# Landing times of loads in a list scheduler, priority for the first batch, and keys loaded ahead of w_out

## The chip, the cores and the metric

The kernel runs on one core of a Trainium2 chip. Times are device microseconds (us) of one execution; "median" is over several executions. A profile is one execution. The engines are TensorE (PE in the profile; PEld is its weight load), VectorE (DVE), ScalarE (ACT), GpSimd (POOL) and SyncE (SP, which issues most loads).

## The reference, cut to what matters

Sketched linear attention of 4 batches, 4 heads, 1088 tokens, head width 32, whose output feeds an MoE-like layer of width 2048 with a rational activation:

```python
def phi(x):                      # q and k: [4, 4, 1088, 32], S1 and S2: [8, 32]
    a = np.einsum('rd,bhsd->bhsr', S1, x)
    b = np.einsum('rd,bhsd->bhsr', S2, x)
    return np.einsum('bhsi,bhsj->bhsij', a, b).reshape(*x.shape[:-1], r * r)
kv = np.einsum('bhsf,bhsd->bhfd', k_p, v);  z = np.sum(k_p, axis=2)
num = np.einsum('bhsf,bhfd->bhsd', q_p, kv)
den = np.einsum('bhsf,bhf->bhs', q_p, z)[..., None] + 1e-06        # x = num / den
...
h = x @ w_in                     # x: [4352, 128], w_in: [128, 2048]
P = a[0] + a[1] * h + a[2] * h2 + a[3] * h3
Q = 1.0 + np.abs(b[0]) * np.abs(h) + np.abs(b[1]) * h2
out = (P / (Q + 1e-06)) @ w_out
```

Nothing of the MoE can start before the first x, and the first x needs the key sums kv of a whole batch.

## The kernel before

Every piece of work is a step with an engine, a guessed duration, what it waits for, a rank, and the buffers it takes and gives back. A small list scheduler plays the steps through and then issues all instructions in the order of the starts that it found. That order is the order of every engine's queue. The guessed times have no other effect; what a step really waits for is settled on the chip.

```python
HOP = 200
...
        t = free_at.get(s["engine"], 0)
        for a in s["after"]:
            t = max(t, a["end"] + (a["lag"] if a["engine"] == s["engine"] else self.HOP + a["lag"]))
        ...                                        # buffers
        key = (t, s["rank"], s["n"])
        if best is None or key < best[0]:
            best = (key, s)
...
def load(fn, ns, n=1, queue="SP", **kw):
    return plan.add(queue, 500 * n, fn, lag=ns, **kw)

ld["kr"] = load(lambda: load_rem(k_rem, k, nc.scalar), 2500, 4, queue="ACT", rank=-98)
...
ld["vr"] = load(lambda: load_rem(v_rem, v, nc.sync), 2500, 4, rank=-95)
ld["ab"] = load(load_ab, 14000, 2, rank=-93)
ld["wi"] = load(lambda: nc.sync.dma_start(out=w_in_sb, in_=moe_w_in), 8000, rank=-92)
ld["wo"] = load(lambda: nc.sync.dma_start(out=w_out_f, in_=...), 9000, rank=-91, take=["L"])
for i, (name, src) in enumerate((("k", k), ("v", v), ("q", q))):       # batch 1
    ld[name, 1] = load(lambda name=name, src=src: load_main(name + "_sb", src, 1), 6000, rank=-90 + i,
                       take=[name + "_sb"])
```

In the head (before the MoE) TensorE also runs matmuls of zeros between the real ones ("warm"). POOL copies v into v_aug (v beside a column of ones) and converts w_out to bf16. In the MoE each group of 128x512 blocks of h goes through eight DVE steps: m = |h|, u = b1*m + b0, u *= m, y = a3*h + a2, y *= h, y += a1, y *= h, y *= r.

## Time and profile before

Median 309.33 us (308.29, 309.33, 309.43). The execution that was profiled took 312.64; its span is 310.9.

| stretch of the profiled execution | length | DVE busy | granted TensorE clock |
|---|---|---|---|
| head, to the first MoE step m<-hb | 41.58 | 9.68 | 0.79 |
| the rest | 269.32 | 258.73 | 0.95 |

First the page of the kernel before. A digit is the busy share of one fortieth of the span in tenths; PEclk is the granted TensorE clock in tenths.

```profile
span 310.9 us, 3191 instructions
PE   7879999999999998998999899989999699866471
DVE  0503269899999999999999999999999999999991
PEclk9995589999999999999999799999999779979667
```

The digits of the last line begin right behind its label. DVE is nearly full from the seventh slice (of 7.8 us) to the last but one, and the clock is at half in the fourth and fifth. So the kernel is bound by DVE after 41.6 us, and everything before is a chain of latencies.

The wait in the head, from the timeline of the kernel before (start, duration, engine, line, operation, output<-input; in brackets the engine's idle time before it and what ended it):

```profile
10.93 0.76 SPq L177 DMA_DIRECT2D L<-in_moe_w_out_dram  x1
11.73 4.59 SPq L138 DMA_DIRECT2D k_sb<-in_k_dram  x1
...
19.86 0.27 ACT L367 COPY kv_low<-kv_ps 64x132 f32<-64x132 f32 x1 [2.33 <-PE kv_ps L358]
20.44 0.58 ACT L271 COPY fT<-w_ps 128x512 f32<-128x512 f32 x1 [0.32 <-PE w_ps L266]
23.21 0.58 ACT L271 COPY fT<-w_ps 128x512 f32<-128x512 f32 x1 [2.19 <-PE w_ps L266]
23.82 0.30 ACT L374 COPY kv_dup<-kv_dup 64x132 f32<-64x132 f32 x1
...
22.52 1.09 PE L266 MATMUL w_ps<-ident,k_sb 128*128 128x128 f32 x8 [2.12 <-DMA k_sb<-in_k_dram]
23.85 1.97 PE L276 MATMUL w_ps<-S_102,fT 128*128 128x64 f32 x8 [0.24 <-ACT fT L271]
25.61 1.92 PE L414 MATMUL h_ps<-kv_dup,q_pT 128*128 128x66 f32 x8
...
41.58 0.43 DVE L494 TENSOR_SCALAR m<-hb 128x1024 int16<-128x1024 int16 x1 [3.53 <-ACT hb L490]
```

The keys of batch 1 (k_sb) are issued behind w_out, and the issue itself blocks SP's queue for 4.59 us. They land at 22.5. In ScalarE's queue the copy of their transposes (fT, 23.21) stands ahead of the last copy into kv_dup (23.82), which batch 0's num/den matmuls (25.61) need. TensorE's queue holds them up further: the transposes (22.52) and the first projection (23.85) of batch 1's keys stand ahead of num/den, which start 1.5 us after kv_dup is done. So batch 0 waits for batch 1's data twice: the scheduler, which guessed a landing 6 us after issue, thought that they were there.

The clock in that time, from windows of the same trace (start:end, length, then busy time and instruction count of PE, PEld, DVE, ACT, POOL, the granted clock, the DMA share and GB/s):

```profile
20.00:24.00 4.00, 1.65 (x13) 1.17 (x11) 0.36 (x2) 1.47 (x4) 0.00 (x0) 0.94 1.12 329
24.00:28.00 4.00, 4.00 (x19) 3.91 (x20) 1.59 (x3) 0.88 (x3) 1.14 (x2) 0.50 0.89 270
36.00:40.00 4.00, 4.00 (x9) 2.23 (x9) 0.63 (x2) 0.27 (x1) 0.00 (x0) 0.50 0.00 0
```

TensorE had little to do from 20 to 24 us, and its clock was at 0.50 from 24 to 40. The Trainium skill says in "TensorE: Matmul & The Clock Gate" (Part 1, the HAM clock gate) that the clock is halved by default and released by activity, in free-running windows of about 3.4 us. This trace agrees with the two levels and with the fall after a thinly used stretch.

### The profile page before, as it was taken

The page shows a single profiled execution, that of the slowest core. Times are in us where ns is not written, and L with a number is a line of the kernel's source. Part 1 is how long each engine was busy: PE and PEld are TensorE (multiplying, and loading weights), DVE is VectorE, ACT ScalarE, POOL GpSimd, SP SyncE. Part 2 cuts the span into 40 slices and gives each one's busy share as a digit, 9 for nine tenths or more (in the row PEclk, how much of TensorE's full clock was granted, in tenths as well). Part 3 has the DMA queues.
Part 4 walks back from the last instruction along what each step waited for, and adds up shares of the span by engine and source line. Part 5 has one row for each costly group of instructions (what it writes and reads, how often), then busy time and mean ns, then how long its engine had stood idle before and what let it go on. Part 6 is the DMA issues. An engine that isn't in the chain of part 4 may idle for free.

```text
span 310.9 us, 3191 instructions
## 1 busy us (share of the span) xinstructions
PE 276.9 (89%) x1247; PEld 166.6 (54%) x1247; DVE 268.4 (86%) x233; ACT 234.4 (75%) x248; POOL 11.0 (4%) x26
## 2 busy tenths in 40 slices
PE   7879999999999998998999899989999699866471
PEld 3769745665546564664546357645645444543150
DVE  0503269899999999999999999999999999999991
ACT  3222259759999888979995899597987996899460
POOL 3103300010000000000000000000000000000000
PEclk9995589999999999999999799999999779979667
DMA  7699100000200000000000000000000000000010
GB/s 215 166 325 300 61 0 3 1 0 0 70 0 34 2 0 34 0 2 0 34 0 2 0 34 3 0 0 34 3 0 0 34 2 0 34 0 0 0 36 17
DMA packets 12655, 11.22 MB, mean 36 GB/s; under 512 B 4065, under 2 KB 10977, under 8 KB 12513
## 3 DMA queue, kind: packets, MB, share of 16 engines
q1 hardware_dynamic: 11472, 10.88, 11.2%
q10 hardware_dynamic: 1168, 0.14, 0.3%
q8 instruction: 10, 0.16, 0.2%
q14 instruction: 5, 0.03, 0.0%
HBM read 8.79 MB, written 2.23 MB: 35 GB/s over the span
## 4 chain that ended last, share of the span: by engine, by line
DVE 67%; PE 12%; ACT 6%; issue 5%; DMA 5%; SPq 2%; DVEq 0%
DVE y L521 20%; DVE y L528 10%; DVE u L504 9%; DVE y L517 6%; DVE y L524 6%; DVE u L500 5%; DVE m L494 5%; PE h_ps L484 4%; DVE f_p L291 4%; DMA k_sb<-in_k_dram 3%; PE out_ps L535 3%; ACT L L508 2%; DMA v_sb<-in_v_dram 2%; DVE x_sb L441 2%; PE w_ps L276 1%
## 5 line engine op out<-in xcount | busy, mean ns | idle before, releaser
L484 PE MATMUL h_ps<-xT,w_in_sb 128*128 128x512 f32 (+1 forms) x288 | 131.9, 596 | 0.2
L490 ACT CAST hb<-h_ps 128x1024 bf16<-128x1024 f32 x68 | 67.6, 1017 | 22.7 <-PE h_ps L484 22.7
L484 PEld LDWEIGHTS h_ps<-xT,w_in_sb 128*128 128x128 f32 x288 | 55.4, 201 | 47.0 <-issue 39.7
L521 DVE TENSOR_TENSOR y<-y,hb 128x4096 bf16<-128x4096 bf16 (+2 forms) x42 | 78.9, 1879 | 0.2
L508 ACT ACTIVATE L<-u,one_ap 128x2048 f32<-128x2048 bf16 (+1 forms) x36 | 69.2, 1921 | 6.4 <-DVE u L504 6.3
L513 ACT ACTIVATE r<-L 128x2048 bf16<-128x2048 f32 (+1 forms) x36 | 65.8, 1827 | 0.5
L535 PE MATMUL out_ps<-r,w_out_103 128*128 128x512 bf16 (+1 forms) x144 | 36.2, 380 | 9.5 <-ACT r L513 9.3
L535 PE MATMUL out_ps<-y,w_out_104 128*128 128x512 bf16 (+1 forms) x144 | 37.0, 403 | 7.9 <-DVE y L528 7.9
L528 DVE TENSOR_TENSOR y<-y,r 128x4096 bf16<-128x4096 bf16 (+2 forms) x21 | 39.5, 1879 | 1.0 <-ACT r L513 0.9
L504 DVE TENSOR_TENSOR u<-u,m 128x4096 bf16<-128x4096 bf16 (+2 forms) x21 | 39.5, 1879 | 0.0
L291 DVE TENSOR_TENSOR f_p<-a_t,w_ps 128x1024 f32<-128x1024 f32 (+1 forms) x16 | 18.9, 1182 | 15.0 <-ACT a_t L283 15.0
L535 PEld LDWEIGHTS <-w_out_103 128*128 128x128 bf16 x144 | 14.7, 103 | 28.3 <-issue 18.4
L535 PEld LDWEIGHTS <-w_out_104 128*128 128x128 bf16 x144 | 15.1, 107 | 25.1 <-issue 14.7
L494 DVE TENSOR_SCALAR m<-hb 128x4096 int16<-128x4096 int16 (+2 forms) x21 | 21.4, 1018 | 3.5 <-ACT hb L490 3.5
L517 DVE TENSOR_SCALAR y<-hb,a_sb 128x4096 bf16<-128x4096 bf16 (+2 forms) x21 | 23.9, 1138 | 0.0
L500 DVE TENSOR_SCALAR u<-m,b_abs 128x4096 bf16<-128x4096 bf16 (+2 forms) x21 | 23.9, 1137 | 0.0
L524 DVE TENSOR_SCALAR y<-y,a_sb 128x4096 bf16<-128x4096 bf16 (+2 forms) x21 | 22.6, 1078 | 0.2
L276 PEld LDWEIGHTS w_ps<-S_102,fT 128*128 128x128 f32 x128 | 17.9, 209 | 4.4 <-issue 2.1
L276 PE MATMUL w_ps<-S_102,fT 128*128 128x64 f32 x128 | 18.4, 290 | 0.8 <-DVE f_p L291 0.6
L336 PEld LDWEIGHTS kv_ps<-v_aug,f_p 128*128 128x128 f32 x128 | 15.8, 192 | 2.4 <-issue 1.6
L414 PEld LDWEIGHTS w_ps<-kv_dup,q_pT 128*128 128x128 f32 x112 | 14.7, 202 | 4.3 <-issue 2.6
L336 PE MATMUL kv_ps<-v_aug,f_p 128*128 128x66 f32 x128 | 15.6, 271 | 0.0
(77 smaller groups left out, 181.4 us busy)
## 6 DMA issues: line engine op xcount, KB each, us to landing
v_sb<-in_v_dram SPq DMA_DIRECT2D x4, 512.0 KB, 5.4
q_sb<-in_q_dram SPq DMA_DIRECT2D x4, 512.0 KB, 6.0
out_dram<-oT SPq DMA_DIRECT2D x8, 256.0 KB, 2.0
k_sb<-in_k_dram SPq DMA_DIRECT2D x3, 512.0 KB, 6.3
w_in_sb<-in_moe_w_in_dram SPq DMA_DIRECT2D x1, 1024.0 KB, 6.2
k_sb<-in_k_dram SPq DMA_DIRECT2D x2, 256.0 KB, 3.3
k_rem<-in_k_dram ACTq DMA_DIRECT2D x4, 32.0 KB, 5.2
v_rem<-in_v_dram SPq DMA_DIRECT2D x4, 32.0 KB, 2.3
```

The lines of the kernel that those rows point to most:

```text
L276: nc.tensor.matmul(T["ab", key][:, i * 64:(i + 1) * 64], lhsT=T["fT", key][:, i * 128:(i + 1) * 128], rhs=S12.rearrange("p h r -> p (h r)" ...
L484: nc.tensor.matmul(T["h", g, s][:, i * W:(i + 1) * W], lhsT=w_in_sb[:, fi * 128:(fi + 1) * 128], rhs=T["xT", n][:, :W], start=True, stop=True)
L490: nc.scalar.copy(out=T["hb", g][:, s * W:(s + nsub) * W], in_=T["h", g, s])
L500: nc.vector.tensor_scalar(out=T["u", g][:, :gw], in0=T["m", g][:, :gw], scalar1=b_abs[:, 1:2], scalar2=b_abs[:, 0:1], op0=AX.mult, op1=AX.add)
L504: nc.vector.tensor_mul(out=T["u", g][:, :gw], in0=T["u", g][:, :gw], in1=T["m", g][:, :gw])
L508: nc.scalar.activation(out=T["L", g, l0][:, :lw], in_=T["u", g][:, l0:l0 + lw], func=ACT.Ln, bias=one_ap)
L513: nc.scalar.activation(out=T["r", g][:, l0:l0 + lw], in_=T["L", g, l0][:, :lw], func=ACT.Exp, scale=-1.0)
L517: nc.vector.tensor_scalar(out=T["y", g][:, :gw], in0=T["hb", g][:, :gw], scalar1=a_sb[:, 3:4], scalar2=a_sb[:, 2:3], op0=AX.mult, op1=AX.add)
L521: nc.vector.tensor_mul(out=T["y", g][:, :gw], in0=T["y", g][:, :gw], in1=T["hb", g][:, :gw])
L524: nc.vector.tensor_scalar(out=T["y", g][:, :gw], in0=T["y", g][:, :gw], scalar1=a_sb[:, 1:2], scalar2=None, op0=AX.add)
L528: nc.vector.tensor_mul(out=T["y", g][:, :gw], in0=T["y", g][:, :gw], in1=T["r", g][:, :gw])
L535: nc.tensor.matmul(T["o", n][:, :W], lhsT=W_terms[t][:, fis[i], :], rhs=src[:, i * W:(i + 1) * W], start=(t == 0 and fis[i] == 0), stop=(t ...
```

## The change

The intent: let the scheduler know when a load really lands, let the steps of the first batch go first, and bring batch 1's keys in sooner. No arithmetic changes. The core of the diff:

```diff
     HOP = 200
+    HURRY = 700
...
-                    t = max(t, a["end"] + (a["lag"] if a["engine"] == s["engine"] else self.HOP + a["lag"]))
+                    t = max(t, a["lands"], a["end"] + (a["lag"] if a["engine"] == s["engine"] else self.HOP + a["lag"]))
...
-                key = (t, s["rank"], s["n"])
+                key = (t - (self.HURRY if s["rank"] < -1 else 0), s["rank"], s["n"], t)
...
-    def load(fn, ns, n=1, queue="SP", **kw):
-        return plan.add(queue, 500 * n, fn, lag=ns, **kw)
+    def load(fn, lands, n=1, queue="SP", **kw):
+        return plan.add(queue, 500 * n, fn, lag=2000, lands=lands, **kw)
...
-    ld["kr"] = load(lambda: load_rem(k_rem, k, nc.scalar), 2500, 4, queue="ACT", rank=-98)
+    ld["kr"] = load(lambda: load_rem(k_rem, k, nc.scalar), 9500, 4, queue="ACT", rank=-98)
...
-    ld["ab"] = load(load_ab, 14000, 2, rank=-93)
-    ld["wi"] = load(lambda: nc.sync.dma_start(out=w_in_sb, in_=moe_w_in), 8000, rank=-92)
+    ld["wi"] = load(lambda: nc.sync.dma_start(out=w_in_sb, in_=moe_w_in), 14500, rank=-94)
+    ld["ab"] = load(load_ab, 15500, 2, rank=-93)
+    ld["k", 1] = load(load_next(1, 0), 17500, rank=-92, take=["k_sb"])
     ld["wo"] = load(lambda: nc.sync.dma_start(out=w_out_f, in_=...),
-                    9000, rank=-91, take=["L"])
+                    21000, rank=-91, take=["L"])
+    ld["v", 1] = load(load_next(1, 1), 23000, rank=-90, take=["v_sb"])
+    ld["q", 1] = load(load_next(1, 2), 25000, rank=-89, take=["q_sb"])
```

`load_next(b, i)`, defined in a part cut here, loads the keys, values or queries of batch b. Before, a load's landing was guessed as a time after its planned issue (`lag`); now `lands` gives it as a time in the plan, before which nothing that needs the load may start. HURRY lets a step whose rank is below -1 go ahead of any step that could start up to 0.7 us sooner. Such ranks have the loads, the first batch's keys and first queries, and the first matmuls of the MoE.

Three parts, then: landing times, priority (HURRY), and load order. Because the scheduler decides everything, each of them moves instructions through the whole kernel.

More of the change, by code (lines that the diff above doesn't have):

```diff
@@ L28, in __init__, with add @@
         self.bufs = bufs
-    def add(self, engine, ns, fn, after=(), rank=0.0, take=(), give=(), lag=0):
+    def add(self, engine, ns, fn, after=(), rank=0.0, take=(), give=(), lag=0, lands=0):
         s = dict(engine=engine, ns=ns, fn=fn, after=[a for a in after if a is not None], rank=rank,
-                 take=take, give=give, lag=lag, end=None, n=len(self.steps))
+                 take=take, give=give, lag=lag, lands=lands, end=None, n=len(self.steps))
         self.steps.append(s)
@@ L56, in issue @@
                     continue
-                key = (t, s["rank"], s["n"])
+                key = (t - (self.HURRY if s["rank"] < -1 else 0), s["rank"], s["n"], t)
                 if best is None or key < best[0]:
                     best = (key, s)
-            (t, _, _), s = best
+            (_, _, _, t), s = best
             for b in s["take"]:
@@ L162, in load_ab @@
                                                 ap=[[0, 128]] + list(moe_b.ap)))
-    def load(fn, ns, n=1, queue="SP", **kw):
-        return plan.add(queue, 500 * n, fn, lag=ns, **kw)
-    ld = {}
-    ld["s"] = load(load_small, 2000, 2, queue="ACT", rank=-99)
-    ld["kr"] = load(lambda: load_rem(k_rem, k, nc.scalar), 2500, 4, queue="ACT", rank=-98)
-    ld["k", 0, 0] = load(lambda: load_main("k_sb", k, 0, 0), 2800, rank=-99, take=["k_sb"])
-    ld["k", 0, 1] = load(lambda: load_main("k_sb", k, 0, 1), 3500, rank=-98)
@@ L172 @@
-    ld["v", 0] = load(lambda: load_main("v_sb", v, 0), 5000, rank=-97, take=["v_sb"])
-    ld["q", 0] = load(lambda: load_main("q_sb", q, 0), 6000, rank=-96, take=["q_sb"])
-    ld["vr"] = load(lambda: load_rem(v_rem, v, nc.sync), 2500, 4, rank=-95)
-    ld["ab"] = load(load_ab, 14000, 2, rank=-93)
-    ld["wi"] = load(lambda: nc.sync.dma_start(out=w_in_sb, in_=moe_w_in), 8000, rank=-92)
-    ld["wo"] = load(lambda: nc.sync.dma_start(out=w_out_f, in_=moe_w_out.rearrange("(fo fi) d -> fi fo d", fi=128)),
-                    9000, rank=-91, take=["L"])
@@ L179, with load_next @@
-    for i, (name, src) in enumerate((("k", k), ("v", v), ("q", q))):
-        ld[name, 1] = load(lambda name=name, src=src: load_main(name + "_sb", src, 1), 6000, rank=-90 + i,
-                           take=[name + "_sb"])
-    ld["qr"] = load(lambda: load_rem(q_rem, q, nc.sync), 3000, 4, rank=-80)
+    def load(fn, lands, n=1, queue="SP", **kw):
+        return plan.add(queue, 500 * n, fn, lag=2000, lands=lands, **kw)
+    def load_next(b, i):
+        name, src = (("k_sb", k), ("v_sb", v), ("q_sb", q))[i]
+        return lambda: load_main(name, src, b)
@@ new lines @@
+    ld = {}
+    ld["s"] = load(load_small, 3000, 2, queue="ACT", rank=-99)
+    ld["kr"] = load(lambda: load_rem(k_rem, k, nc.scalar), 9500, 4, queue="ACT", rank=-98)
+    ld["k", 0, 0] = load(lambda: load_main("k_sb", k, 0, 0), 4000, rank=-99, take=["k_sb"])
+    ld["k", 0, 1] = load(lambda: load_main("k_sb", k, 0, 1), 4900, rank=-98)
+    ld["v", 0] = load(lambda: load_main("v_sb", v, 0), 7200, rank=-97, take=["v_sb"])
+    ld["q", 0] = load(lambda: load_main("q_sb", q, 0), 8900, rank=-96, take=["q_sb"])
@@ new lines @@
+    ld["vr"] = load(lambda: load_rem(v_rem, v, nc.sync), 10700, 4, rank=-95)
+    ld["wi"] = load(lambda: nc.sync.dma_start(out=w_in_sb, in_=moe_w_in), 14500, rank=-94)
+    ld["ab"] = load(load_ab, 15500, 2, rank=-93)
+    ld["k", 1] = load(load_next(1, 0), 17500, rank=-92, take=["k_sb"])
+    ld["wo"] = load(lambda: nc.sync.dma_start(out=w_out_f, in_=moe_w_out.rearrange("(fo fi) d -> fi fo d", fi=128)),
+                    21000, rank=-91, take=["L"])
+    ld["v", 1] = load(load_next(1, 1), 23000, rank=-90, take=["v_sb"])
@@ L183 @@
+    ld["q", 1] = load(load_next(1, 2), 25000, rank=-89, take=["q_sb"])
+    ld["qr"] = load(lambda: load_rem(q_rem, q, nc.sync), 27000, 4, rank=-80)
     for b in range(2, B):
-        for i, (name, src) in enumerate((("k", k), ("v", v), ("q", q))):
-            ld[name, b] = load(lambda name=name, src=src, b=b: load_main(name + "_sb", src, b), 5000, rank=-70 + i,
-                               take=[name + "_sb"])
+        for i, name in enumerate("kvq"):
+            ld[name, b] = plan.add("SP", 500, load_next(b, i), lag=6000, lands=29000 + 2000 * i, rank=-70 + i,
+                                   take=[name + "_sb"])
```

## The prediction

> **What bounds the kernel now.** The profiled span is 310.9 us (median time 309.33). The chain of work that ended last is 67% VectorE (DVE). By stretches: DVE is busy 15.27 of 16.42 us from 41.58 to 58, 229.6 of 232 from 58 to 290, and 13.83 of 20.9 in the tail. Before 41.58, where the first elementwise step of the MoE (m<-hb) starts, it is busy only 9.7 us. So it is DVE-bound from 41.6 us on, and the head is a latency chain; only a shorter head pays much.
>
> **What makes the head long (timeline, chain of waits).**
> 1. The first key sums reach PSUM at 19.82; kv_low and kv_dup follow by 20.5. But ScalarE's next step in order is the copy fT of batch 1's keys, whose load (issued 11.73, behind w_out) lands at 22.48. The last copy into kv_dup runs only at 23.82, and the first num/den matmuls start at 25.61.
> 2. TensorE had nothing to do from 20.41 to 22.52. The granted clock drops to 0.50 by 24 us and stays there until about 41. The Trainium skill ("TensorE: Matmul & The Clock Gate", part on the HAM clock gate) says that idleness halves the clock in windows of about 3.4 us; here 2.1 us of full idleness, in a thinly used stretch, was enough. Num/den then take 1.71 us instead of about 1.0, one 512-wide pass 0.85 instead of 0.43.
> 3. Before x's transposes TensorE does batch 0's second query transposes (L398) and a batch 1 projection: x_sb is done at 30.46, its transposes start at 33.28.
> 4. Earlier, the k_rem transpose holds TensorE 1.29 us for its load (8.48).
>
> **What the change does.** Order only; no arithmetic changes. In the built program, the kv_dup copy on ScalarE directly follows kv_low; k_rem's transpose comes after the first kv matmuls; after num/den only one projection precedes the x transposes; batch 1's keys are issued before w_out, right behind w_in.
>
> Costed with durations of the trace: key projection starts near 7.2 instead of 8.64; kv sums end near 18 (19.82); kv_dup done near 19; batch 1 keys should land near 17 to 17.5 (w_in's 6.2 us from about 9.2, then half its bytes), before TensorE needs them. Num/den start near 19.3 (25.61), x_sb done near 22.4 (30.46), x transposes 22.6, xT 23.8, first h pair 1.7 us at full clock, cast 1.0: first m near 27 (41.58). All 14.5 us of this lie on the critical path. DVE then has about 260.5 us left (268.4 minus about 8; before, 9.7 were done by then), plus idle like before (10.6 us) plus about 0.5. Span: 27 + 260.5 + 11 = 298.5, i.e. 12.5 us less. Time: about 297 us.
>
> **Chances.** 80% range 293 to 302.5. Faster by over 2%: 0.92; within 2%: 0.07; slower: 0.01.
>
> **What would show it right.** First num/den near 19 to 20 us; granted clock 1.0 through 20 to 40 us; first m<-hb at 26 to 28; DVE busy total unchanged near 268 and nearly gapless afterwards; tail as before.
>
> **What would make it wrong.** The clock still drops around 22 to 24 us (only about 2.4 of 3.4 us are filled there): first m near 30, gain about 9. Batch 1's keys land later than 19: same effect. TensorE enters the DVE-bound stage with about 3.5 us less attention work done in advance, and it is nearly full until 240 us: DVE could starve some us. The later order, rescheduled everywhere, may lose or win 1 to 2 us.

## The result, and the profile after

Median 301.36 us (300.58 to 302.09, 4 runs) against 308.81 of the kernel before in the same rounds; ratio 0.976, 95% interval 0.972 to 0.979. This ratio is the mean time of one kernel's fast runs over that of the other's in the same rounds, so not quite the ratio of the medians quoted. The time predicted, 297, was 4.4 us too low; the range to 302.5 held it. All outputs are right.

The page of the kernel after (its profiled execution took 301.32):

```profile
span 299.5 us, 3180 instructions
PE   8999899999899989999999899998989979593642
DVE  0436989999999999999999999999999999999990
PEclk9999999999999999999999999999999999988675
```

DVE is nearly full from the fifth digit to the last but one, and the clock no longer falls in the head. The same wait in the timeline after:

```profile
10.99 0.49 SPq L140 DMA_DIRECT2D k_sb<-in_k_dram  x1
11.69 0.76 SPq L185 DMA_DIRECT2D L<-in_moe_w_out_dram  x1
...
17.86 0.27 ACT L374 COPY kv_low<-kv_ps 64x132 f32<-64x132 f32 x1 [1.66 <-PE kv_ps L365]
18.55 0.30 ACT L381 COPY kv_dup<-kv_dup 64x132 f32<-64x132 f32 x1 [0.42 <-DVE kv_dup L378]
18.88 1.07 ACT L278 COPY fT<-w_ps 128x512 f32<-128x512 f32 x2
...
18.90 2.16 PE L421 MATMUL h_ps<-kv_dup,q_pT 128*128 128x66 f32 x16
26.30 0.43 DVE L501 TENSOR_SCALAR m<-hb 128x1024 int16<-128x1024 int16 x1 [2.63 <-ACT hb L497]
```

kv_dup is copied right after kv_low, num/den start at 18.90 (predicted: near 19.3), the first m<-hb is at 26.30 (predicted: near 27). The head is as foreseen. But the head is 15.3 us shorter than in the profile before, the span only 11.4, and the median only 7.5. Three things ate the difference, and the following sum shows them. It holds in every trace by construction, since the idle time is what is left:

span = time of the first m<-hb + DVE's busy time after it + DVE's idle time after it.

| trace | span | first m<-hb | DVE busy before it | DVE busy in all | busy after it | idle after it |
|---|---|---|---|---|---|---|
| before (312.64 us) | 310.9 | 41.58 | 9.68 | 268.42 | 258.74 | 10.58 |
| b_again, the same kernel (308.42 us) | 306.6 | 38.41 | 9.68 | 268.19 | 258.51 | 9.68 |
| after (301.32 us) | 299.5 | 26.30 | 7.84 | 270.30 | 262.46 | 10.74 |

First, the profile before is that of a slow execution for this kernel (its state on record is fast: 312.64 is 1.4% above the fastest run, and slow begins at 1.5%); a second trace of the same kernel (next section) has its first m<-hb at 38.41. Against that one the head gains 12.1 us. Second, 3.95 us more DVE work comes after that point: 1.84 us was done in the head before and is not now (one product f_p, 1.22, and one reciprocal with its division, 0.62), and 2.11 us is new. Third, DVE idles 1.06 us more after that point. The 2.11 us are three tensor_scalar steps that became long. From the timeline after, first DVE, then POOL:

```profile
26.65 1.27 DVE L524 TENSOR_SCALAR y<-hb,a_sb 128x1024 bf16<-128x1024 bf16 x1
27.84 0.53 DVE L507 TENSOR_SCALAR u<-m,b_abs 128x1024 bf16<-128x1024 bf16 x1
29.49 1.26 DVE L531 TENSOR_SCALAR y<-y,a_sb 128x1024 bf16<-128x1024 bf16 x1
56.26 1.86 DVE L531 TENSOR_SCALAR y<-y,a_sb 128x4096 bf16<-128x4096 bf16 x1
```

```profile
26.37 1.26 POOL L317 TENSOR_SCALAR v_aug<-v_sb 128x1024 f32<-128x1024 f32 x1
29.26 1.21 POOL L317 TENSOR_SCALAR v_aug<-v_sb 128x1024 f32<-128x1024 f32 x1 [1.25 <-DMA v_sb<-in_v_dram]
53.79 3.26 POOL L317 TENSOR_SCALAR v_aug<-v_sb 128x1024 f32<-128x1024 f32 x1
```

The same y<-hb step takes 0.54 in the kernel before, where POOL's first two copies of v (24.14 and 29.18) ran while DVE was still waiting for the MoE. Each long step begins while a POOL copy is under way and ends 0.3 to 1.1 us after that copy. The third copy took 3.26 us itself, not 1.04: DVE multiplications of two tensors ran until 56.13 (one was ending when the copy began, the next took 2.28 us), and then the copy held up the tensor_scalar step at 56.26.

### The profile page after: what moved, and what is told of

It reads as the page before. It is cut to its first block, busy times and chain, and to the rows that moved or that the text cites. A ratio compares the mean times of both kernels' runs of the same rounds, so it can differ in the third digit from the quotient of the medians.

```text
span 299.5 us, 3180 instructions
## 1 busy us (share of the span) xinstructions
PE 263.5 (88%) x1228; PEld 156.2 (52%) x1247; DVE 270.3 (90%) x233; ACT 234.2 (78%) x248; POOL 13.8 (5%) x26
## 4 chain that ended last, share of the span: by engine, by line
DVE 78%; issue 7%; ACT 5%; DMA 4%; PE 3%; SPq 1%; DVEq 0%
DVE y L528 22%; DVE y L535 12%; DVE u L511 11%; DVE y L524 7%; DVE m L501 7%; DVE y L531 6%; DVE u L507 6%; DVE f_p L298 4%; DVE x_sb L448 2%; DMA b_sb<-in_moe_b_dram 2%; ACT L L515 2%; DMA v_sb<-in_v_dram 2%; ACT hb L497 2%; PE h_ps L421 1%; PE h_ps L491 1%
## 5 line engine op out<-in xcount | busy, mean ns | idle before, releaser
L491 PE MATMUL h_ps<-xT,w_in_sb 128*128 128x512 f32 (+1 forms) x288 | 127.0, 576 | 0.8 <-ACT xT L460 0.7
L491 PEld LDWEIGHTS h_ps<-xT,w_in_sb 128*128 128x128 f32 x288 | 52.5, 192 | 44.5 <-issue 38.1
L542 PE MATMUL out_ps<-y,w_out_104 128*128 128x512 bf16 (+1 forms) x137 | 34.9, 388 | 12.5 <-DVE y L535 12.0
L542 PE MATMUL out_ps<-r,w_out_103 128*128 128x512 bf16 (+1 forms) x134 | 35.3, 377 | 10.0 <-ACT r L520 9.0
L542 PEld LDWEIGHTS <-w_out_104 128*128 128x128 bf16 x144 | 14.6, 102 | 31.9 <-issue 21.0
L542 PEld LDWEIGHTS <-w_out_103 128*128 128x128 bf16 x144 | 14.3, 101 | 27.6 <-issue 18.5
L524 DVE TENSOR_SCALAR y<-hb,a_sb 128x4096 bf16<-128x4096 bf16 (+2 forms) x21 | 24.6, 1172 | 0.0
L531 DVE TENSOR_SCALAR y<-y,a_sb 128x4096 bf16<-128x4096 bf16 (+2 forms) x21 | 24.0, 1143 | 0.2
L283 PEld LDWEIGHTS w_ps<-S_102,fT 128*128 128x128 f32 x128 | 16.7, 191 | 3.5 <-issue 1.4
L283 PE MATMUL w_ps<-S_102,fT 128*128 128x64 f32 x128 | 16.3, 269 | 0.0
L421 PEld LDWEIGHTS w_ps<-kv_dup,q_pT 128*128 128x128 f32 x112 | 13.8, 192 | 3.5 <-issue 3.3
```

The source lines that it names most:

```text
L491: nc.tensor.matmul(T["h", g, s][:, i * W:(i + 1) * W], lhsT=w_in_sb[:, fi * 128:(fi + 1) * 128], rhs=T["xT", n][:, :W], start=True, stop=True)
L524: nc.vector.tensor_scalar(out=T["y", g][:, :gw], in0=T["hb", g][:, :gw], scalar1=a_sb[:, 3:4], scalar2=a_sb[:, 2:3], op0=AX.mult, op1=AX.add)
L531: nc.vector.tensor_scalar(out=T["y", g][:, :gw], in0=T["y", g][:, :gw], scalar1=a_sb[:, 1:2], scalar2=None, op0=AX.add)
L542: nc.tensor.matmul(T["o", n][:, :W], lhsT=W_terms[t][:, fis[i], :], rhs=src[:, i * W:(i + 1) * W], start=(t == 0 and fis[i] == 0), stop=(t ...
```

## The experiments

Twelve runs were made; two of them repeat the kernels before and after. "b_" kernels are edits of the kernel before, "a_" of the kernel after. The sums of all traces, computed as above:

| trace | first m<-hb | busy before | DVE busy in all | idle after | span | median us | ratio to before (95%) |
|---|---|---|---|---|---|---|---|
| b_again | 38.41 | 9.68 | 268.19 | 9.68 | 306.6 | 308.80 | 0.997 (0.989 to 1.005) |
| b_swap | 33.16 | 9.50 | 268.40 | 10.14 | 302.2 | 304.49 | 0.983 (0.975 to 0.992) |
| b_warm | 35.11 | 9.50 | 268.02 | 10.37 | 304.0 | 305.51 | 0.986 (0.976 to 0.996) |
| a_swap | 35.25 | 7.84 | 268.96 | 11.33 | 307.7 | 310.44 | 1.002 (0.993 to 1.010) |
| a_nohurry | 31.40 | 9.50 | 268.21 | 10.49 | 300.6 | 301.25 | 0.972 (0.967 to 0.977) |
| a_oldlag | 29.38 | 7.83 | 272.83 | 12.02 | 306.4 | 307.61 | 0.993 (0.987 to 0.998) |
| a_actv | 26.25 | 7.83 | 268.38 | 12.70 | 299.5 | 301.86 | 0.973 (0.968 to 0.978) |
| a_pool3 | 26.42 | 7.84 | 273.44 | 12.68 | 304.7 | 306.35 | 0.989 (0.984 to 0.995) |
| a_vdma | 27.15 | 7.83 | 268.84 | 11.44 | 299.6 | 300.75 | 0.980 (0.974 to 0.986) |
| a_nowarm | 29.54 | 7.75 | 269.31 | 10.60 | 301.7 | 303.76 | 0.988 (0.980 to 0.996) |
| a_vdma_nowarm (slow run) | 34.92 | 7.85 | 268.60 | 11.83 | 307.5 | 308.64 | none (slow runs) |
| a_again | 27.05 | 7.84 | 269.69 | 10.80 | 299.7 | 301.54 | 0.977 (0.973 to 0.981) |

Rounds ran on different chips, so medians of different rows are compared with care; rows of one call are b_again to a_swap, a_nohurry to a_pool3, a_vdma to a_vdma_nowarm, and a_again alone. The ratios of the first four rows can't be rebuilt from the runs listed as fast: their means give 1.000, 0.987, 0.990 and 1.005, some 0.4 points higher, with the same order.

### The kernel before, once more: b_again

No edit.

> The kernel before, unchanged, for a second trace. The profile of before (312.64 us) was 1.2% slower than its median (308.8). Theory: executions differ in when the granted clock of TensorE drops and recovers in the head, so here the mean clock is above 0.928, the first m<-hb lies about 3 us earlier than 41.58, and the run is near 308.8. Rival: the spread comes from the DVE-bound stage; then the first m<-hb stays within 1 us of 41.58 and the rest of the span is shorter. Ratio to before 1.00.

The profiled execution took 308.42, the clock over it was 0.942 instead of 0.928, and the first m<-hb came at 38.41:

```profile
24.00:28.00 4.00, 4.00 (x20) 3.78 (x19) 1.08 (x1) 1.57 (x4) 1.14 (x2) 0.50 0.79 253
28.00:32.00 4.00, 3.78 (x19) 3.72 (x19) 1.73 (x7) 0.41 (x1) 2.55 (x2) 0.50 1.07 352
32.00:36.00 4.00, 3.32 (x24) 2.62 (x24) 1.32 (x2) 1.88 (x5) 2.31 (x2) 0.98 0.18 59
```

Here the clock is back by 32 us; in the first trace it was still at 0.50 at 40. That explains 3.2 of the 4.3 us between the two spans; the rest is 0.9 us of idle time later on and 0.2 of busy time. So the theory held for these two traces: the kernel before is slower or faster with the moment at which the clock recovers. Of 49 executions of it 38 lie between 307.0 and 310.4 us, nine between 312.6 and 314.2 (the profiled one among them), and two at 304.1 and 304.6. The nine have a mean clock of 0.922 to 0.928, all others whose clock is on record 0.931 or more.

Read in steps of 0.1 us, the clock was at half for 17.07 us in the first trace (23.5 to 40.6) and for 10.24 us here (21.9 to 32.1): five times and three times 3.41 us. The same holds of every half-clock stretch of the other traces in the first 44 us: 3.41 us in b_swap and a_nohurry and twice in a_oldlag, 6.83 in a_pool3, 10.24 in a_nowarm, 13.65 in a_swap, 23.89 in a_vdma_nowarm. So in these traces a clock that fell came back only after whole stretches of 3.41 us. Why it took five of them in one execution and three in the other is not settled by these runs.

### Only the load order, in the kernel before: b_swap

```diff
-    ld["wo"] = load(lambda: <load w_out>, 9000, rank=-91, take=["L"])
+    ld["wo"] = load(lambda: load_main("k_sb", k, 1), 9000, rank=-91, take=["L"])
...                                                    # and the step of batch 1's keys loads w_out
```

The two steps exchange what they load, so that the plan, and with it every other queue, stays as it was.

> The kernel before with one thing changed: batch 1's keys are issued ahead of w_out; every other instruction stands in its old order. Theory (the head was long because of the wait for this load): the keys land near 17.5, the kv_dup copy runs near 21.5 instead of 23.8, num/den start near 22 at full clock, first m<-hb near 31.6 instead of 41.58, granted clock 1.0 from 20 to 40 us; time 300 to 304. Rival (the new order of the steps makes the gain): first m<-hb not under 38, time above 306.

From its timeline:

```profile
22.57 0.30 ACT L376 COPY kv_dup<-kv_dup 64x132 f32<-64x132 f32 x1
23.54 2.11 PE L416 MATMUL h_ps<-kv_dup,q_pT 128*128 128x66 f32 x16
33.16 0.81 DVE L496 TENSOR_SCALAR m<-hb 128x1024 int16<-128x1024 int16 x1 [1.78 <-ACT hb L492]
```

kv_dup was copied at 22.57 (b_again: 24.54), the clock was 1.00 from 20 to 40 us, the first m<-hb came at 33.16: 5.3 us earlier than in b_again. The span fell by 4.4 and the ratio is 0.983. The direction and the clock are as the theory said, the head 1.6 us later than it said. Of these, 0.9 us lie before the wait: in this execution the clock had already been at 0.50 from 9.4 to 12.8 us, and kv_low came at 20.88 instead of 20.00 in b_again, on the same chip. The wait for the keys was real and worth roughly five of the twelve microseconds.

### Only the load order taken back, in the kernel after: a_swap

```diff
-    ld["k", 1] = load(load_next(1, 0), 17500, rank=-92, take=["k_sb"])
+    ld["k", 1] = load(lambda: <load w_out>, 17500, rank=-92, take=["k_sb"])
-    ld["wo"] = load(lambda: <load w_out>, 21000, rank=-91, take=["L"])
+    ld["wo"] = load(load_next(1, 0), 21000, rank=-91, take=["L"])
```

> The kernel after with one thing changed: w_out is issued ahead of batch 1's keys again; every other instruction stands in after's order. Theory (load): TensorE waits for the keys until about 22.5, is idle for some 4 us, the clock drops, first m<-hb near 33 to 36 instead of 26.3, time 304 to 308. Rival (order): first m<-hb below 29, time below 303.

From its timeline, what TensorE and DVE waited for:

```profile
22.11 1.09 PE L273 MATMUL w_ps<-ident,k_sb 128*128 128x128 f32 x4 [3.23 <-DMA k_sb<-in_k_dram]
35.25 0.43 DVE L501 TENSOR_SCALAR m<-hb 128x1024 int16<-128x1024 int16 x1 [4.83 <-ACT hb L497]
```

TensorE stood still 3.23 us before the keys' transposes, because the new order also puts those ahead of num/den, and the clock was at 0.50 from 21.7 to 35.3. The head is as the load theory said, the time worse: 310.4, not distinguishable from the kernel before, although its first m<-hb is 3.2 us earlier than b_again's. The sum says what took these 3.2 us back, and 1.1 more: 1.84 of DVE work moved out of the head, 0.77 more DVE time in all, 1.65 of more idle time. So the new order is worth nothing without the early keys. It is a plan for landing times, and where they don't come true it is no better than the old one.

### Only the clock: b_warm

```diff
                                  stop=True, skip_group_check=True)
+            if b == 0:
+                warm(8)
```

> The kernel before with 8 idle matmuls (1.7 us) put on TensorE right after the first key sums, in the time in which it waits for batch 1's keys. Nothing waits for them. Theory (the clock's drop is a large part of the long head): clock stays at 1.0 from 20 to 40 us, kv_dup is still copied near 23.8, first m<-hb near 33.5 instead of 41.58, time 301 to 304. Rival (only the wait itself counts): less than 2 us of gain, time above 306.5.

The clock stayed at 1.00 from 20 to 40 us:

```profile
20.00:24.00 4.00, 3.00 (x19) 1.99 (x20) 0.36 (x2) 0.94 (x3) 0.00 (x0) 1.00 1.10 333
24.00:28.00 4.00, 3.76 (x33) 3.42 (x32) 1.89 (x5) 1.55 (x4) 1.14 (x2) 1.00 0.77 220
36.00:40.00 4.00, 4.00 (x16) 2.09 (x14) 3.90 (x9) 3.24 (x5) 0.00 (x0) 1.00 0.00 0
```

kv_dup was still copied late (24.52), but the first m<-hb came at 35.11 instead of 38.41, the ratio is 0.986, and all four runs lie between 304.8 and 306.2. The gain was below what was expected (301 to 304), since a typical run of the kernel before loses less to the clock than the profiled one. So the fall of the clock alone costs about 3.3 us of the head in a typical execution: eight useless matmuls that nobody waits for take 1.4% off the kernel by the ratio (1.0% by the means of the fast runs).

### Only the priority taken out: a_nohurry

```diff
-    HURRY = 700
+    HURRY = 0
```

> The kernel after without the priority for the first batch's steps (HURRY 0); landing times and load order as after. The keys land early, but TensorE then does both transposes and a projection of batch 1's keys before num/den, and the second query transposes before x. Theory (priority is worth some 4 us of the head, as the distance from b_swap to after suggests): first m<-hb near 30.5 to 32, time 303 to 305. Rival (early landing does nearly all): first m<-hb below 28, time within 1 us of 301.4.

The first m<-hb came at 31.40, as the theory said, and the time was 301.25, as the rival said: both fell short, because both took a shorter head for a shorter kernel. The sum against the trace of after: the head is 5.1 us longer, but DVE did 1.66 us more before it, lost nothing to POOL (268.21 busy instead of 270.30: both of POOL's early copies of v ran before the MoE began), and idled 0.25 less. Of 5.1 us of shorter head 4.0 are given back, and the medians don't tell the two kernels apart. Nor are the 5.1 us all due to the order. The page of a_nohurry shows the clock falling in the fourth slice:

```profile
PEclk9997999999999999999998999999999699979577
```

It was at 0.50 from 26.5 to 29.9 us. Up to the start of the first pass of h 3.7 us were lost (26.92 against 23.24), and 1.4 more in that pass, at half clock. The profiled execution was also the slowest of the four (302.35), so its head is no typical one.

### Only the landing times taken out: a_oldlag

```diff
-    def load(fn, lands, n=1, queue="SP", **kw):
-        return plan.add(queue, 500 * n, fn, lag=2000, lands=lands, **kw)
+    def load(fn, ns, n=1, queue="SP", **kw):
+        return plan.add(queue, 500 * n, fn, lag=ns, **kw)
...                                                    # with the old lags; order and HURRY as after
```

> The kernel after with the old model of the loads (lag after issue) but the new load order and the priority. k_rem's transpose stands early again, and POOL copies v of batches 1 and 2 before it converts w_out. Theory: TensorE waits for k_rem at 8.5 us again, first m<-hb near 27.5 to 28.5; POOL's w_out conversions now run inside the DVE-bound stage, so DVE busy rises to 271 to 274; time 302.5 to 305. Rival (the landing times are worth nothing beside order and priority): time within 1 us of 301.4.

The first m<-hb came at 29.38. TensorE waited 1.60 us for k_rem before 8.70 again, the clock was at 0.50 from 9.7 to 13.1, and kv_low came at 20.94 instead of 17.86, which is the whole of the 3.1 us that this head is longer than after's. Further, DVE's busy time is 4.6 us above b_again's, above all for two steps and what POOL did beside them:

```profile
30.54 2.19 DVE L524 TENSOR_SCALAR y<-hb,a_sb 128x1024 bf16<-128x1024 bf16 x1
32.66 2.11 DVE L507 TENSOR_SCALAR u<-m,b_abs 128x1024 bf16<-128x1024 bf16 x1
...
30.32 2.13 POOL L253 TENSOR_SCALAR w_out<-L,a_sb 128x2048 bf16<-128x2048 f32 x1
32.42 2.06 POOL L254 TENSOR_SCALAR w_out<-L 128x2048 bf16<-128x2048 f32 x1
```

With the old lags, POOL copies v of batches 1 and 2 first and waits for the second of these loads until 29.3; the conversions of w_out come after it, in the midst of the first MoE steps, which take 2.1 to 2.2 us instead of 0.54. At 307.6 us it was slower than expected: it gains 0.7% on the kernel before, where the whole change gains 2.4. Taken out of the whole change one at a time, then, the landing times cost some 6 us and the priority nothing that the medians show (both against 301.4 on another chip). The landing times without the other two parts were not run.

### POOL against DVE: a_actv and a_pool3

a_actv lets ScalarE do the copies of v of batches 1 to 3, at the same place of the plan; a_pool3 lets POOL do each of them three times.

```diff
-            nc.gpsimd.tensor_scalar(out=T["va", b][:, :, :, 0:D], in0=T["v_sb", b], ...)
+            nc.scalar.copy(out=T["va", b][:, :, :, 0:D], in_=T["v_sb", b])        # a_actv, b > 0
+            for _ in range(1 if b == 0 else 3):                                   # a_pool3
+                nc.gpsimd.tensor_scalar(out=T["va", b][:, :, :, 0:D], in0=T["v_sb", b], ...)
```

> The kernel after with one thing changed: the copy of v into v_aug of batches 1 to 3 runs on ScalarE instead of POOL, at the same place of the order. Theory (a POOL instruction that reads SBUF blocks DVE's tensor_scalar steps: three of them took 1.27, 1.26 and 1.86 us instead of 0.54, 0.48 and 1.29): these three are back at 0.54, 0.48 and 1.29, DVE busy 268.2 instead of 270.3, time 299 to 300.3 (after: 301.4) unless ScalarE's three extra microseconds show. Rival (the three long steps have another cause, such as traffic of the loads): they stay long and time stays at 301 or above.

> The kernel after with POOL's copy of v into v_aug done three times over in batches 1 to 3 (six more POOL instructions of about 1.04 us, same result). Nobody waits for POOL longer than some us, with slack. Theory (shared access of POOL and DVE): more long tensor_scalar steps, about 0.6 to 0.8 us lost for each added POOL instruction, DVE busy 273 to 276 instead of 270.3, time 304 to 306.5. Rival: DVE busy stays within 0.5 us of 270.3 and time within 1 us of 301.4.

With POOL's copies gone, DVE's busy time is 268.38, that of the kernel before, and none of the three steps is long any more. With three times as many, it is 273.44: nine copies cost 5.2 us over 268.2, three cost 2.1, so 0.6 to 0.7 us each. The time rises by some five microseconds: 3.1 of more DVE busy time and 1.9 of more idle time, the latter in an execution whose clock was at half for 6.8 us from 35.6 on. In a_pool3 steps with two tensor inputs were caught as well:

```profile
28.01 1.26 DVE L508 TENSOR_SCALAR u<-m,b_abs 128x1024 bf16<-128x1024 bf16 x1
29.78 1.53 DVE L512 TENSOR_TENSOR u<-u,m 128x1024 bf16<-128x1024 bf16 x1
```

(0.53 and 0.68 when alone.) The rule behind it is in the Trainium skill, "SBUF — State Buffer", section "Who interferes with whom": DVE and GpSimd share one pair of SBUF ports as an exclusive lock, which a tensor_scalar in a 2-port performance mode needs, and a step with two SBUF inputs needs against a GpSimd step that reads SBUF; the later one "fully blocks". These traces agree: no long step ends before POOL's instruction does. It then needs a little less than its usual time: the steps at 26.65, 29.49 and 56.26 end 0.29, 0.28 and 1.07 us after the copy, where alone they take 0.54, 0.48 and 1.29.

a_actv still did not win: its idle time after the head rose by 1.96 us, to 12.70, and the span is the same 299.5. From its timeline:

```profile
53.68 1.03 ACT L321 COPY v_aug<-v_sb 128x1024 f32<-128x1024 f32 x1
61.80 1.23 DVE L504 TENSOR_SCALAR m<-hb 128x4096 int16<-128x4096 int16 x1 [1.82 <-ACT hb L500]
```

DVE now waits 1.82 us for a cast of h on ScalarE at 61.8, where it waited 0.33 in the kernel after. The two traces side by side show what delays it there. The timeline marks no gap on ScalarE from 52.84 (after) or 51.77 (a_actv) to that cast. It starts 1.07 us ahead in a_actv, does the extra copy of 1.03, and has the cast at 60.75 against 60.87, only 0.12 ahead, while DVE was 1.6 us ahead. So the wait grew by 1.5 us, 1.0 of it for the copy and the rest because DVE's lead was larger than ScalarE's. The other 0.5 of the 1.96 us is not traced.

### Trying for more: a_vdma, a_nowarm and both

a_vdma loads v of batches 1 to 3 straight into v_aug, in runs of 128 bytes; a_nowarm leaves out the 12 zero matmuls between the real ones in the head.

```diff
+        for h in range(H):                                                        # a_vdma, b > 0
+            nc.sync.dma_start(out=T["va", b][:, h, :, 0:D], in_=src[:, h])
-        warm_n = 1 if b == 0 else 0                                               # a_nowarm, both places
+        warm_n = 0
```

> A version meant to beat both: the kernel after, but batches 1 to 3 load v straight into v_aug (runs of 128 bytes, four loads per batch, behind the query load), so that neither POOL nor ScalarE copies it and POOL only writes the column of ones. Theory: first m<-hb stays at 26.3, the three long tensor_scalar steps go back to 0.54, 0.48 and 1.29, DVE busy 268.2, idle after the first m stays at 10.5 to 11.5 (unlike a_actv with 12.7), time 299 to 300 against 301.4 of after. It fails if the loads of short runs land later than about 45 us: then DVE idles in 45 to 65 us.

> The kernel after without the 12 idle matmuls between the real ones in the head (the 8 at the start stay), so that TensorE, busy 12.3 of 12.9 us from 4.9 to 17.8, gets through the head sooner. If TensorE's own work bounds the head and the clock stays up: first m<-hb near 24 instead of 26.3, but POOL's w_out conversions (22.5 to 26.4) now meet the first DVE steps, DVE busy 271 to 273, time 299.5 to 301.5. If these matmuls are what keeps the clock up: granted clock falls below 0.9 before 26 us and first m<-hb is at 27 or later, time 302 to 305.

> Both of the last two changes together. If each does what its theory says, first m<-hb near 24 and no collision with v's copies, but still with the w_out conversions: time 297.5 to 299.5. If the clock falls, 301 to 304.

a_vdma took away the long steps but the first: w_out's conversions, which ended at 27.9 in this execution, still caught the first m<-hb (1.01 us instead of 0.43). Median 300.75 (300.15 to 301.78). Its ratio of 0.980 is not to be trusted, as two runs of the kernel before at 304 us in these rounds made most of its normal runs count as slow; the same holds of a_nowarm's 0.988, from the same rounds. No run puts it against the kernel after on one chip. By its median it is 0.6 us better than the kernel after (0.8 than a_again), within the spread of both.

a_nowarm fits the view that the zero matmuls keep the clock up:

```profile
16.00:20.00 4.00, 2.59 (x20) 2.28 (x19) 0.56 (x4) 1.81 (x6) 0.00 (x0) 0.92 0.93 289
20.00:24.00 4.00, 4.00 (x19) 3.60 (x18) 1.85 (x6) 0.27 (x1) 0.00 (x0) 0.50 1.07 318
24.00:28.00 4.00, 3.33 (x5) 1.50 (x5) 0.77 (x1) 0.59 (x1) 3.58 (x2) 0.50 0.82 217
```

num/den start at 18.51, hardly earlier, the clock falls at 19.4, and the first m<-hb is at 29.54; two of its six runs were at 308.3. Why num/den came no earlier is another wait: kv_low was there at 16.78, but in DVE's queue the sum into kv_dup stood behind a step on b_sb (b_abs), whose load landed only at 17.75, so that TensorE idled 1.41 us before num/den. The fall is thus that of fewer matmuls and of this wait together. With both edits the clock was at 0.50 from 9.6 to 33.5 us in the profiled (slow) execution and the runs spread from 303.7 to 309.8: a failure for the same reason, and no test of the sum of the two edits. No version here beats the kernel after beyond doubt.

### The kernel after, once more: a_again

No edit.

> The kernel after, unchanged, for a second trace and a second ratio. If the account of the first trace holds: granted clock 1.0 up to 40 us, first m<-hb at 26 to 27.5, DVE busy 269.5 to 270.5 with two or three tensor_scalar steps lengthened by 0.5 to 0.8 us where a POOL copy of v runs, idle after the first m 10.2 to 11.3, time 300.5 to 302, ratio to before 0.970 to 0.981. If the long steps were an accident of one execution, DVE busy is 268.2 to 268.6.

First m<-hb at 27.05, DVE busy 269.69, ratio 0.977 (0.973 to 0.981). In this execution the MoE began 0.75 us later, and POOL's copies fell on other steps: m<-hb took 0.60, u<-m at 31.01 took 1.27 instead of 0.53, y<-y at 56.39 again 1.87. So the collisions come back, at the steps that happen to meet a copy.

## Why the prediction was right or wrong

- "The kernel is DVE-bound from 41.6 us on, and only a shorter head pays": right. In every trace the span is the head plus DVE's work plus 10 to 13 us of idle time.
- "First m near 27", "num/den start near 19.3", "granted clock 1.0 through 20 to 40 us": right (26.30 and 27.05; 18.90; 1.00).
- The wait for batch 1's keys and the fall of the clock as the two causes: right, each shown by itself. Early keys alone shorten the head by 5.3 us (b_swap), the clock kept up alone by 3.3 (b_warm). The two are not independent, since the early keys also keep the clock up. For the rest of the 12.1 us the prediction named two more points (3 and 4), the steps ahead of x's transposes and the wait for k_rem. Both went as foreseen: the x transposes start at 21.96 (predicted 22.6), and k_rem's comes at 13.06 without a wait. No run takes out one of these two alone. Taking out the priority gives 5.1 us of the head back, taking out the landing times 3.1; each includes a fall of the clock, so these parts do not add up to a sum.
- "DVE then has about 260.5 us left": wrong by 2.0. It had 262.46. The 1.8 us no longer done in the head were in the sum (9.7 against 8); the 2.1 us lost to POOL were not. The prediction even named "DVE busy total unchanged near 268" as a sign, and it was 270.3. The step that failed is the belief that order changes no durations: a shorter head lets DVE's fast steps meet POOL copies that used to run beside an idle DVE.
- "Plus idle like before (10.6) plus about 0.5": right (10.74). "Span 298.5": 299.5. That it is only 1.0 off is in part luck: the head came 0.7 us earlier than predicted and the idle time was 0.3 less, which hides half of the 2.0 us above.
- "12.5 us less. Time: about 297": this is the step that cost most. The saving was computed from a profile of an execution of 312.64 us and taken from a median of 309.33 us. Taken from 312.64 it gives 300.1. The profile's head (41.58) held a long time at half clock which most executions don't have (38.41 in the second trace). That is 3.3 of the 4.4 us of error; the wrong span is 1.0 more. "All 14.5 us lie on the critical path" was true of that execution and of few others.
- Of the risks named, the clock's fall did not happen with the whole change, but it did in the variants that loosened the head: a_swap, a_nowarm, and for 3.4 us each a_nohurry, a_oldlag and b_swap. TensorE's lost advance of 3.5 us did not starve DVE in the kernel after: idle time after the head is 1.1 us above b_again's, and 0.7 of that lies in the last 20.9 us.

Left open: why the clock recovers so differently between executions of the kernel before, and what the landing times are worth without the other two parts.

## What to carry to other kernels

Before a saving read from a profile is taken off a time, compare the profiled execution's own time with the median. A shorter latency chain at the start of a throughput-bound kernel is paid back in part: count what the bottleneck engine used to do in that time, and what other engines did beside it while it was idle (here POOL's copies), for both now come on top. In this kernel, whose order is planned ahead, true landing times were worth more than the priority (307.6 us without the former, 301.3 without the latter), and a plan built on a landing that didn't come true was worth nothing (a_swap, ratio 1.002).

## What the Trainium skill lacked or had wrong

- "TensorE: Matmul & The Clock Gate": it gives about 3.4 us of activity for the release of the clock. In the two traces of the kernel before TensorE was busy nearly all the time from 24 us on (4.00 of 4 us from 24 to 28; in the first trace with projections and num/den matmuls from 23.85 to 29.6), yet the clock was at 0.50 for 17.07 us in one and 10.24 us in the other. The length of a window agrees: all half-clock stretches read here are whole multiples of 3.41 us. The page's part on the clock gate has no figure for how much filling keeps the clock up. These runs give no threshold either: it held through 4 us with 3.00 (b_warm, from 20) and with 2.44 (b_again, from 4) us of TensorE work, and it fell in 4 us with 1.65 (before, from 20), with 2.59 (a_nowarm, from 16) and even with 3.33 (a_nohurry, from 24).
- "SBUF — State Buffer": the exclusive lock is as these traces show it; the page has no figure for what a DVE step loses to a GpSimd copy. Here a POOL copy of 128x1024 fp32 (1.04 us alone) costs DVE 0.6 to 0.7 us on average, and a 2.1 us conversion turns a 0.54 us step into one of 2.1 to 2.2.
- "DMA: Bandwidth & Descriptors": it does not say that an issue can block the issuing queue behind earlier loads. Here the issue behind the w_out load (1 MB in runs of 512 bytes) held SP's queue for 4.59 us before and 5.29 us after, and the loads after it were issued that much later (4.40 us in a_swap, 5.04 in b_swap; issues of the same size elsewhere took about 0.5). That the earlier loads' backlog is the reason is not shown apart.
